# Moving a 32-column multiply from VectorE to GpSimd, and shifting a PSUM tile by eight columns

## The chip, the cores and the metric

The kernel runs on one core of a Trainium2 chip. A core has five engines that each run their own list of instructions in order and meet only through semaphores: TensorE (PE, matrix products), VectorE (DVE), ScalarE (ACT), GpSimd (POOL) and SyncE (SP, which here issues nearly all DMAs). The metric is the device time of one execution in microseconds, as a median of several; smaller is better.

## The reference

The input x is 2048 tokens by 640 features. After a layer norm without weights, two branches are added to x: a linear attention with 32 heads of 20 features ("hedgehog" feature maps), and a gated MLP of width 1536.

```python
xn = layernorm(x)
q, k, v = split(xn @ wqkv)                          # 32 heads of 20
pq, pk = q @ w_phi[h], k @ w_phi[h]                 # per head
phi_q = concat([softmax(pq), softmax(-pq)])         # 40 features per head
phi_k = concat([softmax(pk), softmax(-pk)])
kv  = sum_s phi_k[s, f] * v[s, d];   z = sum_s phi_k[s, f]
num = phi_q @ kv;   den = phi_q @ z + 1e-6
out = x + (num / den) @ wo + (silu(xn @ w1) * (xn @ w3)) @ w2
```

There is no mask: kv and z are sums over all tokens, so they must be complete before the first query is multiplied with them.

## The kernel before, in words

**Tiles.** Tokens lie in 16 tiles of 128 (index t). All matrices are bf16 and PSUM is f32: 8 banks of 512 columns, used as four pairs. `w_phi` is folded into the key and query weights first (`Wkp`, `Wqp`), so each projection gives the argument of the exponentials.

**Keys and values.** For each tile `k_tile` projects, ScalarE writes exp(p) and exp(-p) interleaved by head into `ekt`, and `k_norm` makes both softmaxes: VectorE sums the groups of 20 and takes reciprocals, GpSimd multiplies `ekt` by them in two instructions of 640 columns (`ekt<-ekt,rS`). `kv_sum` then multiplies `ekt` with v, which has a column of ones per head and so 21 columns per head, in 11 groups of up to three heads (the trace calls it `PS<-v,ekt`, 11 matmuls per tile). `kv_store` masks the result into `KVc`, 32 x 21 columns.

**Queries.** `q_proj` (`PS<-Wqp,xnT`, ten matmuls) and ScalarE's exponentials fill `eq`, where three heads of 40 features plus 8 pads make a group of 128. `q_half` (GpSimd, where the planner finds GpSimd free) adds the two halves of each softmax's terms into `half`; `q_ratio` (line 642) sums on VectorE (`Sq`: per head the sum of exp(p) and the sum of exp(-p)), takes the reciprocal of the second sum (`rq`), and multiplies it by the first, in line 650. `q_scale` (line 652) multiplies the exp(-p) terms by that ratio on GpSimd, in two instructions of 600 and 40 columns, so that both softmaxes share one denominator. A transposing DMA on SP's queue turns `eq` into `eqT`.

**The products with kv.** `q_tok` (line 664) multiplies the 11 groups of `eqT` with their 63 (last: 42) columns of `KVc`, side by side from column 0 of a pair of banks. One bank holds 512 columns and eight groups take 504, so group 8 crosses into the second bank at its eighth column. A matmul writes to one bank only, so this group is issued twice, with 8 and 55 columns: 12 matmuls per tile (`PS<-KVc,eqT`). VectorE then forms the denominator, its reciprocal and `o_tok`; SP transposes it to `oT`.

**The rest.** `mlp` (line 683) issues ten 512-column matmuls per block of 128 hidden features (`PS<-xnT,w_s`), a tanh on ScalarE (`th`), and on VectorE `t<-th,PS` and `hT<-t,PS`, both of which read the PSUM pair and so free it. `out_tile` adds `wo` and `w2` products in PSUM; VectorE adds x (`xres`) and SP stores.

**What sets the order.** The kernel writes its instruction lists with a planner. Each stage is a stream; at every turn the head of each stream is given a start time from costs written beside each operation (`cost=`), and the earliest one is committed, with its PSUM pair (`banks`, line 723) chosen by when it comes free. From then on all five lists are fixed, and waits are derived from the recorded reads and writes. A changed cost or engine anywhere can therefore reorder all that comes after it. The planner knows nothing of one engine slowing another. All operations but DMAs are issued from line 102, so the profile's rows are told apart by their tile names.

Of the kernel before, what the change touches and what calls it, by code (L numbers as in the profile page):

```python
# [4 lines left out]
ALU = mybir.AluOpType  # L5
# [5 lines left out]
H = 32  # L11
# [6 lines left out]
NG = 11  # L18
# [231 lines left out]
def bass_parallel_sum__linear_kernel_hedgehog__glu_gated_swiglu__prompt_kernel(  # L250
# [29 lines left out]
    def new(name, shape, dtype, offset=None):  # L280
        size = mybir.dt.size(dtype)
        for n in shape[1:]:
            size *= n
        return P.sbuf(name, shape, dtype, region(size) if offset is None else offset)
# [39 lines left out]
    eqT = [new(f"eqT{i}", [128, NG, 128], bf, (RKV, RE + 27648)[i // 2] + 5632 + 2816 * (i % 2)) for i in range(4)]  # L324
# [8 lines left out]
    KVc = new("KVc", [128, H * 21], bf, RW)  # L333
# [6 lines left out]
    PS = nc.alloc_psum_tensor("PS", [128, 8 * 512], f32)  # L340
# [3 lines left out]
    def bank(k, cols=512, off=0, rows=128):  # L344
        return PS[0:rows, k * 512 + off:k * 512 + off + cols]
# [5 lines left out]
    def mm(o, l, r, start, stop, shared=False, cost=None):  # L351
        n = free(r)
        P.op("PE", "matmul", [o], [l, r], (o, l, r),
             dict(start=start, stop=stop, skip_group_check=shared),
             cost=max(n / 2400 + 0.003, 0.055) if cost is None else cost)
# [5 lines left out]
    def free(ap):  # L361
        n = 1
        for s in ap.shape[1:]:
            n *= s
        return n
# [5 lines left out]
    def tt(eng, o, a, b, f, fast=1):  # L371
        c = 0.16 + free(o) / 960 / fast if eng == "DVE" else 0.2 + free(o) * 1.7 / 1000
        P.op(eng, "tensor_tensor", [o], [a, b], (o, a, b, f), cost=c)

    def stt(o, a, s, b, f0, f1):
        P.op("DVE", "scalar_tensor_tensor", [o], [a, b], (),
             dict(out=o, in0=a, scalar=s, in1=b, op0=f0, op1=f1), cost=0.16 + free(o) / 960)
# [206 lines left out]
    def group(g):  # L584
        return 3 * g, min(3, H - 3 * g)
# [46 lines left out]
    def q_sums(t):  # L632
        s = Sq[:, t % 4, :]
        i = eq[t % 4][:].rearrange("p (g c) -> p g c", c=128)[:, :, 0:120].rearrange("p g (n f) -> p g n f", f=DH)
        h = half[:, t % 2, :].rearrange("p (g n f) -> p g n f", n=6, f=10)
        return s[:, 0:66].rearrange("p (g n) -> p g n", n=6), i, h
# [5 lines left out]
    def q_ratio(t, halved):  # L642
        o, i, h = q_sums(t)
        i = h if halved else i
        P.op("DVE", "tensor_reduce", [o], [i], (o, i, AX.X, ALU.add), cost=0.12 + free(i) / 960)
        s = Sq[:, t % 4, :]
        r = rq[:, t % 3, :]
        sv = s[:, 0:64].rearrange("p (h s) -> p h s", s=2)
        P.op("DVE", "reciprocal", [r], [sv[:, :, 1]], (r, sv[:, :, 1]), cost=0.36)
        tt("DVE", r, r, sv[:, :, 0], ALU.mult)  # L650

    def q_scale(t):
        r = rq[:, t % 3, :]
# [10 lines left out]
    def q_tok(t, k):  # L664
        for g in range(NG):
            h, nh = group(g)
            c = 21 * h
            for a, b in ((c, min(c + 21 * nh, 512)), (max(c, 512), c + 21 * nh)):
                if a < b:
                    mm(bank(k, b - a, a), eqT[t % 4][:, g, :], KVc[:, a:b], a in (0, 512), b in (512, 21 * H), True,  # L670
                       max(0.026, (b - a) / 2400 + 0.003))
        p = PS[:, k * 512:k * 512 + 21 * H].rearrange("p (h c) -> p h c", c=21)
        den = den_s[:, t % 2, :]
        sv = Sq[:, t % 4, 0:64].rearrange("p (h s) -> p h s", s=2)
        stt(den, sv[:, :, 0], DEN_EPS, p[:, :, DH], ALU.mult, ALU.add)
        P.op("DVE", "reciprocal", [den], [den], (den, den), cost=0.36)
        tt("DVE", o_tok[:, t % 3, :].rearrange("p (h c) -> p h c", c=DH), p[:, :, 0:DH],
           den.unsqueeze(2).to_broadcast([128, H, DH]), ALU.mult)
# [192 lines left out]
    def q_norms():  # L871
        for t in range(T):
            while done["qp"] <= t:
                yield None
            halved = P.free["POOL"] < P.free["PE"] + 2.0
            if halved:
                yield lambda t=t: q_half(t)
            yield lambda t=t, halved=halved: q_ratio(t, halved)
            yield lambda t=t: q_scale(t)
            done["qn"] = t + 1  # L880
# [8 lines left out]
    def q_toks():  # L889
        for t in range(T):  # L890
            while done["qd"] <= t or not done["kv"]:
                yield None
            yield lambda t=t: q_tok(t, banks(2))
            done["q"] = t + 1
# [129 lines left out]
```

## Time and profile before

| | us |
|---|---|
| median of three runs (lowest, highest) | 271.44 (271.33, 271.71) |
| the profiled execution | 271.57 |
| its span in the profile | 269.8 |

Busy shares of the span: PE 98%, PE's weight loads 60%, VectorE 66%, ScalarE 37%, GpSimd 36%. The granted TensorE clock is full in all 40 slices.

How to read it: times are microseconds from the start of the span. Matmuls are pipelined and their ends are modelled, so the length shown for one (0.38 us for 512 columns) is longer than the distance from one to the next; where the pace of TensorE is wanted, starts are compared. In a row of the timeline stand start, length, engine, line, operation, output and inputs, form, and how many instructions were merged into it ("x40"); some matmul records are missing, so a merged row can say x39 where 40 were issued. A bracket at its end gives the idle time ahead of it and what ended that. Weight loads (PEld) overlap matmuls.

### The profile page before, as it was taken

Reading aid. Unit: us, or ns where it says so; the run is one execution under the profiler, and the core shown is the slowest. Engines: PE = TensorE matmul, PEld = TensorE weight load, DVE = VectorE, ACT = ScalarE, POOL = GpSimd, SP = SyncE. Lnnn points to the kernel's source line nnn. Section 1 sums busy time; section 2 is a strip of 40 time slices with the busy share of each in tenths; the row PEclk is TensorE's granted clock in tenths of the full one; section 3 lists DMA queues with packets and bytes.
Section 4 is the critical chain, followed back from the end, with each engine's and each line's share of the span. In section 5 each row is a group of like instructions: output and inputs, shape, how many; then the busy total and the mean of one; then the engine's idle time right before and its main releaser. Section 6 shows DMA issues by size and latency. Waiting matters only on the chain.

```text
span 269.8 us, 4835 instructions
## 1 busy us (share of the span) xinstructions
PE 263.6 (98%) x1958; PEld 161.9 (60%) x1978; DVE 177.9 (66%) x308; ACT 99.6 (37%) x193; POOL 97.5 (36%) x126
## 2 busy tenths in 40 slices
PE   7999999999989999999999999999999999999996
PEld 4656677776736555555555455544577777777774
DVE  4549899998899898888988878878712121212112
ACT  5547979988323434435242434242100000000000
POOL 4225848999993443644444434222000000000000
PEclk9999999999999999999999999999999999999999
DMA  6998695900093255455444460424211313131301
GB/s 193 282 309 179 147 220 116 308 10 2 4 327 72 49 102 80 80 99 102 87 80 89 91 80 10 93 57 78 49 51 52 97 49 97 51 97 49 93 31 49
DMA packets 63510, 27.73 MB, mean 103 GB/s; under 512 B 49792, under 2 KB 63488, under 8 KB 63488
## 3 DMA queue, kind: packets, MB, share of 16 engines
q1 hardware_dynamic: 63344, 27.35, 43.1%
q8 instruction: 15, 0.25, 0.4%
q10 hardware_dynamic: 144, 0.08, 0.1%
q14 instruction: 7, 0.06, 0.1%
HBM read 12.81 MB, written 2.62 MB: 57 GB/s over the span
## 4 chain that ended last, share of the span: by engine, by line
PE 74%; POOL 12%; DVE 9%; issue 3%; DMA 1%; DVEq 0%
PE PS L102 74%; POOL ekt L102 10%; DVE bst L102 4%; DVE x_tok L102 1%; POOL rstd L102 1%; DVE S L102 1%; DMA x_tok<-in_A_x_dram 1%; POOL v L102 1%; DVE hT L102 1%; DVE t L102 1%; DVE Sq L102 1%; DVE mv L102 0%; DVE rS L102 0%; POOL M L102 0%; DVE xres L102 0%
## 5 line engine op out<-in xcount | busy, mean ns | idle before, releaser
L102 PE MATMUL PS<-xnT,w_s 128*128 128x512 bf16 x463 | 105.8, 379 | 1.9 <-DVE t L102 0.8
L102 PEld LDWEIGHTS PS<-xnT,w_s 128*128 128x128 bf16 x480 | 45.5, 98 | 52.2 <-DVE t L102 1.3
L102 PE MATMUL PS<-w_s,hT 128*128 128x320 bf16 (+2 forms) x384 | 54.9, 299 | 0.0
L102 DVE TENSOR_TENSOR xres<-PS,xres 128x640 bf16<-128x640 f32 (+2 forms) x17 | 13.3, 785 | 60.0 <-PE PS L102 60.0
L102 ACT ACTIVATE th<-PS 128x512 f32<-128x512 f32 x48 | 28.8, 600 | 52.4 <-PE PS L102 52.4
L102 PEld LDWEIGHTS PS<-w_s,hT 128*128 128x128 bf16 x384 | 37.6, 98 | 14.6
L102 DVE SCALAR_TENSOR_TENSOR t<-th,PS 128x512 bf16<-128x512 f32 x48 | 32.7, 681 | 15.0 <-ACT th L102 14.6
L102 POOL TENSOR_TENSOR eq<-eq,rq 128x600 bf16<-128x600 bf16 (+1 forms) x32 | 22.6, 727 | 53.8 <-DVE rq L102 53.7
L102 POOL TENSOR_TENSOR ekt<-ekt,rS 128x640 bf16<-128x640 bf16 x32 | 39.5, 1265 | 0.6 <-DVE rS L102 0.6
L102 ACT ACTIVATE eq<-PS 128x600 bf16<-128x600 f32 (+1 forms) x72 | 24.6, 411 | 27.8 <-PE PS L102 27.6
L102 DVE SCALAR_TENSOR_TENSOR hT<-t,PS 128x512 bf16<-128x512 bf16 x48 | 33.0, 687 | 1.8 <-DVE t L102 0.2
L102 PE MATMUL PS<-wv,xnT 128*128 128x320 bf16 x160 | 24.8, 299 | 0.1
L102 PE MATMUL PS<-wo_s,oT 128*128 128x320 bf16 (+2 forms) x160 | 24.5, 299 | 0.0
L102 PE MATMUL PS<-Wkp,xnT 128*128 128x320 bf16 x160 | 23.9, 299 | 0.0
L102 ACT ACTIVATE ekt<-PS 128x640 bf16<-128x640 f32 x32 | 22.3, 703 | 3.8 <-PE PS L102 3.3
L102 PE MATMUL PS<-Wqp,xnT 128*128 128x128 bf16 (+1 forms) x157 | 23.3, 297 | 0.2
L102 DVE TENSOR_REDUCE S<-ekt 128x64 f32<-128x1280 bf16 x16 | 23.0, 1438 | 0.0
L102 POOL TENSOR_TENSOR half<-eq 128x660 f32<-128x660 bf16 x14 | 19.0, 1356 | 8.6 <-ACT eq L102 8.6
L102 PEld LDWEIGHTS PS<-wo_s,oT 128*128 128x128 bf16 x160 | 15.7, 98 | 6.3
L102 PEld LDWEIGHTS PS<-Wqp,xnT 128*128 128x128 bf16 x160 | 12.9, 98 | 10.7
L102 PEld LDWEIGHTS PS<-wv,xnT 128*128 128x128 bf16 x160 | 15.2, 98 | 6.8 <-DVE xnT L102 0.4
L102 PEld LDWEIGHTS PS<-Wkp,xnT 128*128 128x128 bf16 x160 | 15.5, 98 | 6.0
(55 smaller groups left out, 176.9 us busy)
## 6 DMA issues: line engine op xcount, KB each, us to landing
w_s<-in_B_w_dram SPq DMA_DIRECT2D x6, 640.0 KB, 6.2
xres<-in_A_x_dram SPq DMA_DIRECT2D x16, 160.0 KB, 2.3
out_dram<-xres SPq DMA_DIRECT2D x15, 160.0 KB, 1.8
x_tok<-in_A_x_dram SPq DMA_DIRECT2D x3, 640.0 KB, 6.3
w_s<-in_B_w_dram SPq DMA_DIRECT2D x1, 1920.0 KB, 8.0
wv<-in_A_wqkv_dram SPq DMA_DIRECT2D x2, 400.0 KB, 5.4
wo_s<-in_A_wo_dram SPq DMA_DIRECT2D x1, 800.0 KB, 8.4
x_tok<-in_A_x_dram SPq DMA_DIRECT2D x3, 160.0 KB, 3.3
```

The lines of the kernel that those rows point to most:

```text
L102: o = _Op(eng, lambda: m(*args, **kw), r, w, cost)
```

## The change

Two things, in two functions. In `q_ratio` the multiplication of the reciprocal by the first sum, 32 columns of f32, is issued on GpSimd and not on VectorE. In `q_tok` the output starts at column 8 of the PSUM pair and not at column 0: eight groups then end at column 512, the ninth starts the second bank, no group is split, and a tile takes 11 matmuls. VectorE reads the products from the shifted place. The planner's cost for these matmuls becomes 0.031 each (before: the larger of 0.026 and a value by columns).

```diff
     def q_ratio(t, halved):
         ...
         P.op("DVE", "reciprocal", [r], [sv[:, :, 1]], (r, sv[:, :, 1]), cost=0.36)
-        tt("DVE", r, r, sv[:, :, 0], ALU.mult)
+        tt("POOL", r, r, sv[:, :, 0], ALU.mult)
 ...
     def q_tok(t, k):
         for g in range(NG):
             h, nh = group(g)
-            c = 21 * h
-            for a, b in ((c, min(c + 21 * nh, 512)), (max(c, 512), c + 21 * nh)):
-                if a < b:
-                    mm(bank(k, b - a, a), eqT[t % 4][:, g, :], KVc[:, a:b], a in (0, 512), b in (512, 21 * H), True,
-                       max(0.026, (b - a) / 2400 + 0.003))
-        p = PS[:, k * 512:k * 512 + 21 * H].rearrange("p (h c) -> p h c", c=21)
+            a, b = 21 * h, 21 * (h + nh)
+            mm(bank(k, b - a, 8 + a), eqT[t % 4][:, g, :], KVc[:, a:b], g in (0, 8), g in (7, NG - 1), True, 0.031)
+        p = PS[:, k * 512 + 8:k * 512 + 8 + 21 * H].rearrange("p (h c) -> p h c", c=21)
```

Since the planner places everything anew, the built lists differ in more than these lines. Up to the reciprocal of the first query tile all engines' lists are the same. From there on GpSimd has 16 more multiplications (`rq<-rq,Sq`) and one more `half<-eq`: query tile 1, whose 1320 terms VectorE summed alone before, is now halved first. TensorE's list has the same projections and MLP blocks in a different order, with the 16 kv products at other places between them; SP's transposes of `eqT` and `oT` change places twice.

## The prediction

> **What bounds the kernel now.** The first view to read is the page's busy shares, then who kept TensorE waiting.
>
> ```profile
> PE 263.6 (98%) x1958; PEld 161.9 (60%) x1978; DVE 177.9 (66%) x308; ACT 99.6 (37%) x193; POOL 97.5 (36%) x126
> ...
> PE PS L102 <- DVE warm L102: 1.2, 1, 1.2
> PE PS L102 <- DVE t L102: 0.8, 1, 0.8
> PE PS L102 <- ACT Wkp L102: 0.2, 1, 0.2
> PE PS L102 <- DVE rstd L102: 0.2, 1, 0.2
> ```
>
> TensorE is the bound, and the waits on it are four. Three lie in the start-up, ahead of everything the change touches. The fourth, 0.8 us behind VectorE's `t`, is in the middle. Everything else after start-up is matmul behind matmul. So time can change in two ways only: fewer or shorter matmuls, or waits of TensorE that come or go. The third view is the timeline around that wait.
>
> ```profile
> 65.30 14.77 POOL L102 TENSOR_TENSOR ekt<-ekt,rS 128x640 bf16<-128x640 bf16 x12
> 70.82 0.63 DVE L102 SCALAR_TENSOR_TENSOR t<-th,PS 128x512 bf16<-128x512 f32 x1
> 73.51 6.42 PE L102 MATMUL PS<-xnT,w_s 128*128 128x512 bf16 x29
> 74.07 1.47 DVE L102 TENSOR_REDUCE Sq<-eq 128x66 f32<-128x1320 bf16 x1
> 74.57 0.60 ACT L102 ACTIVATE th<-PS 128x512 f32<-128x512 f32 x1 [4.90 <-PE PS L102]
> 75.57 0.35 DVE L102 RECIPROCAL rq<-Sq 128x32 f32<-128x32 f32 x1
> 75.96 4.16 DVE L102 TENSOR_TENSOR rq<-rq,Sq 128x32 f32<-128x32 f32 x1
> 80.04 0.68 DVE L102 SCALAR_TENSOR_TENSOR t<-th,PS 128x512 bf16<-128x512 f32 x1
> 80.20 1.41 POOL L102 TENSOR_TENSOR eq<-eq,rq 128x600 bf16<-128x600 bf16 x2
> 80.75 0.69 DVE L102 SCALAR_TENSOR_TENSOR hT<-t,PS 128x512 bf16<-128x512 bf16 x1
> 80.77 1.84 PEld L102 LDWEIGHTS PS<-xnT,w_s 128*128 128x128 bf16 x10 [1.33 <-DVE t L102]
> 80.78 2.33 PE L102 MATMUL PS<-xnT,w_s 128*128 128x512 bf16 x10 [0.84 <-DVE t L102]
> 82.94 1.52 PE L102 MATMUL PS<-v,ekt 128*128 128x63 bf16 x44
> ```
>
> The multiplication `rq<-rq,Sq` of query tile 0, 32 columns, takes 4.16 us. How long it takes otherwise stands here, with its neighbours:
>
> ```profile
> L102 DVE TENSOR_TENSOR rq<-rq,Sq x16: 191/192/4160, 76.0 to 181.9; 128x32 f32<-128x32 f32 x16
> ...
> L102 POOL TENSOR_TENSOR eq<-eq,rq 128x40 bf16<-128x40 bf16 x16 | 4.0, 252 | 0.0
> ...
> L102 POOL TENSOR_TENSOR rstd<-rstd 128x2 f32<-128x2 f32 x6 | 1.2, 196 | 0.5
> ```
>
> The long one begins inside GpSimd's run of twelve `ekt` multiplications and ends at 80.12, when that run is over (65.30 + 14.77 = 80.07). The sum (74.07), the reciprocal (75.57) and a `t` (70.82) ran at their usual lengths beside the same GpSimd work. What sets this instruction apart is that both its inputs lie in SBUF; `t` and `hT` have one there and one in PSUM. Behind it in VectorE's list stands the `t` of an MLP block whose tanh was ready at 75.17. It starts at 80.04, its PSUM bank comes free late, and the fourth block of the run of 40 matmuls, which needs that pair, waits.
>
> The Trainium skill, SBUF — State Buffer, "SBUF: two separate sides", has such a rule: a VectorE instruction with two SBUF inputs and a GpSimd instruction that reads SBUF exclude each other, and the later one blocks until the earlier has ended. The trace agrees on which instruction blocks, but the block outlasted three GpSimd instructions of 1.23 us (14.77/12) and not one.
>
> **The change part by part.**
>
> *VectorE's multiplication goes.* Sixteen leave VectorE: 15 x 0.19 + 4.16 = 7.0 us of its time. Fifteen of them are covered, since no matmul waits on VectorE there. The long one is not: without it the first `t` of that stretch can start at about 75.97, and its `hT` ends near 77.4. How long TensorE stood is read from starts. The pace of 512-column matmuls comes from these rows:
>
> ```profile
> 148.55 8.79 PE L102 MATMUL PS<-xnT,w_s 128*128 128x512 bf16 x39
> 157.18 0.52 PE L102 MATMUL PS<-KVc,eqT 128*128 128x63 bf16 x12
> ```
>
> 40 of them (one record is missing) take 157.18 - 148.55 = 8.63 us, 0.216 each. The 29 from 73.51 would be followed by the next at 73.51 + 29 x 0.216 = 79.77; it came at 80.78. The wait cost 1.01 us. The rows' own bounds are 0.84 (PE idle) and 1.33 (PEld idle).
>
> What is late next: the fourth block would start at 79.77 and the `v,ekt` matmuls at 79.77 + 10 x 0.216 = 81.93; their last `ekt` is ready at 80.07, so there are 1.9 us of cover. The second and third `hT` free banks for the projection at 83.3 and the block at 84.65; their tanhs end by 79.5 and VectorE does a `t` and `hT` in 1.4, so they are done by about 81. Nothing in the profile takes the wait's place; I take 1.01.
>
> *GpSimd's multiplication comes.* Its price is between 0.196 (2 columns, f32) and 0.252 (40 columns); by columns 32 lies by the latter, and I take 0.24. Sixteen are 3.9 us, and the additional `half` (1.36) makes 5.2, on an engine that is 36% busy. Behind the new instruction on GpSimd are `q_scale`'s two and the next `half`; behind those SP's transpose and then the kv products. The path from reciprocal to `q_scale` was, for tile 10:
>
> ```profile
> 141.56 0.35 DVE L102 RECIPROCAL rq<-Sq 128x32 f32<-128x32 f32 x1
> 141.94 0.19 DVE L102 TENSOR_TENSOR rq<-rq,Sq 128x32 f32<-128x32 f32 x1
> 142.21 1.42 POOL L102 TENSOR_TENSOR eq<-eq,rq 128x600 bf16<-128x600 bf16 x2 [3.62 <-DVE rq L102]
> 143.66 1.38 SPq L114 DMA_TRANSPOSE eqT<-eq  x1
> ...
> DMA to landing us min/median/max: 3.5/3.6/5.3
> ...
> 148.19 0.52 PE L102 MATMUL PS<-KVc,eqT 128*128 128x63 bf16 x12
> ```
>
> From the reciprocal's end (141.91) to `q_scale` it is 0.30. With the hop to GpSimd first (142.21 - 142.13 = 0.08), then 0.24, and a step on GpSimd of at most another 0.08, it becomes 0.32 to 0.40: up to 0.1 later. `eqT` landed at 143.66 + 3.6 = 147.26, 0.93 ahead of its matmuls. So 0.1 is hidden even here, the closest of the tiles. Had that cover gone, a tile would cost 0.1.
>
> The new order is a second risk to this cover. I count matmuls in the changed list at the paces above. For tiles 4 to 11 there lie 3 projections (10 matmuls, 1.36), 60 large matmuls and 2 kv products between a projection's start and that tile's kv product: 3 x 1.36 + 60 x 0.216 + 2 x 0.34 = 17.7 us. In the order before, tile 10 had 15.6 and still 0.93 to spare. The shortest stretch in both orders is tile 15's, 60 large matmuls with one projection and one product, 14.7 in either; there the rows of before are
>
> ```profile
> 173.93 1.52 PE L102 MATMUL PS<-Wqp,xnT 128*128 128x512 bf16 x10
> 183.65 1.39 SPq L114 DMA_TRANSPOSE eqT<-eq  x1
> 188.60 0.52 PE L102 MATMUL PS<-KVc,eqT 128*128 128x63 bf16 x12
> ```
>
> and `eqT` landed at 187.25, 1.35 early. For tile 0 the product comes at 88.16 (81.93 + 44 x 0.031 + 1.36 + 2.16 + 1.36) and not at 89.18, while GpSimd delivers 0.2 later: transposed from 81.85, landed by 85.5, 2.7 early. For tile 1, now halved on GpSimd and summed by VectorE only behind the `KVc` copies, I get: copies from 83.4 to 84.7, sum and reciprocal to 85.9, GpSimd to 87.6, landed 91.2; its product stands at 88.16 + 0.34 + 20 x 0.216 = 92.8, 1.6 early. So the order costs nothing that I can find.
>
> *One matmul less per tile.* The block of 12 takes about 0.365:
>
> ```profile
> 120.16 0.52 PE L102 MATMUL PS<-KVc,eqT 128*128 128x63 bf16 x12
> 120.53 1.52 PE L102 MATMUL PS<-Wqp,xnT 128*128 128x512 bf16 x10
> ...
> 69.22 4.24 PE L102 MATMUL PS<-v,ekt 128*128 128x63 bf16 x132
> ```
>
> The same shapes as the new block, ten of 63 and one of 42 columns, are the `v,ekt` products of a tile: 132 of them have their starts in 4.24 - 0.18 (the modelled length of the last) = 4.06, 0.031 each, so 11 take 0.34. The difference is 0.025, over 16 tiles 0.40 us, on TensorE's path throughout. Bounds: 0.02 a tile (the two parts of the split group were short ones), 0.32; and a full 0.031, 0.50.
>
> *Sum.* Against the profiled execution, 271.57: 271.57 - 1.01 - 0.40 = 270.16. Outside the span lie 271.57 - 269.8 = 1.8 us, which nothing touches. The median of the runs is 0.13 lower than the profiled one, so 270.0 to 270.2; I say 270.1. With the bounds of both terms, 0.84 + 0.32 and 1.33 + 0.50, and the median as reference, it is 269.6 to 270.4.
>
> **The rivals.**
>
> *The wait stays.* If VectorE was held by something else than this instruction's inputs, the next one in its list would be held instead, and only the matmuls' 0.4 remains: 271.44 - 0.4 = 271.0, no change that can be measured. Against it: three other kinds of VectorE instructions ran beside the same GpSimd work.
>
> *A smaller new wait.* The lists are placed anew by costs that knew nothing of the 4.16 us, and a kv product or a bank may come up to 0.9 late once or twice in 16 tiles: 270.4 to 270.9. For it: margins of 0.93 exist. Against it: TensorE had no other wait in the old order, made from the same costs.
>
> *Slower: the chain through GpSimd.* The multiplication now stands in GpSimd's list ahead of `q_scale`, and each tile's transpose hangs on it. It decides once the chain is more than the margin longer, that is when the small multiplication takes over 0.93 + 0.19 = 1.1 us or so. As long as GpSimd's 640-column one (1.23), it would make tiles with that margin wait 0.2; were all sixteen so close, 3 us, and the time 271.4 - 1.4 + 3 = 273. For it: GpSimd is slow per instruction. Against it: its rows of 0.196 and 0.252, and longer stretches in the new order. The Trainium skill, GPSIMD Engine Reference, "Engine selection", speaks against the change: elementwise work belongs on VectorE, GpSimd being about twice as slow with two inputs. By that rule the instruction takes 2 x 0.19 = 0.38, an estimate from the page, and the chain would be 0.2 longer, still under the margin of 0.93; the sum would be the same.
>
> **How the numbers follow.** A measurement of this kernel can tell about 0.2%, 0.54 us, from no change (its three runs span 0.38). Wait gone and no new one: 0.77, at 270.1 (269.6 to 270.4). A smaller new wait: 0.08, also faster. The wait stays: 0.06, same. Slower by the chain, or by a late bank of that order: 0.09. Faster is 0.85. The range reaches from 269.6 to the smaller new wait's end, 270.9, and leaves 0.15 out.
>
> **What would show it.** Right: no `rq` on VectorE, 16 on GpSimd of 0.2 to 0.3 us; no row of VectorE over 2 us; no wait of TensorE behind `t`; 11 kv matmuls in 0.34 us; the last matmul group starting 1.4 us earlier. Wrong: a wait of TensorE behind `eqT`, `KVc` or `hT` after 76 us; a `t` at 76 that takes 4 us; or `rq` on GpSimd of a microsecond.

## The result, and the profile after

| | before | after |
|---|---|---|
| median of six runs (lowest, highest), us | 271.40 (271.21, 271.71) | 269.91 (269.55, 270.20) |
| profiled execution, us | 271.57 | 269.55 |
| its span, us | 269.8 | 267.8 |

The ratio is 0.9944, with a 95% interval of 0.9931 to 0.9957: faster by 1.49 us (0.6%), as forecast in sign, in size (270.1 was said) and, as the rest shows, in its two causes.

First the busy shares of the changed kernel:

```profile
PE 263.9 (99%) x1962; PEld 161.7 (60%) x1962; DVE 171.0 (64%) x292; ACT 99.5 (37%) x193; POOL 102.9 (38%) x143
```

and all waits of TensorE in it (total, times, longest):

```profile
PE PS L102 <- DVE warm L102: 1.2, 1, 1.2
```

The wait behind `t` is no longer there; what is left is the very first wait of the start-up. VectorE lost 6.9 us of busy time (7.0 was worked out), GpSimd gained 5.4 (5.2). The timeline of the same stretch as before:

```profile
72.67 8.79 PE L102 MATMUL PS<-xnT,w_s 128*128 128x512 bf16 x40
74.95 0.35 DVE L102 RECIPROCAL rq<-Sq 128x32 f32<-128x32 f32 x1
75.22 0.63 DVE L102 SCALAR_TENSOR_TENSOR t<-th,PS 128x512 bf16<-128x512 f32 x1
79.41 0.25 POOL L102 TENSOR_TENSOR rq<-rq,Sq 128x32 f32<-128x32 f32 x1
79.73 1.41 POOL L102 TENSOR_TENSOR eq<-eq,rq 128x600 bf16<-128x600 bf16 x2
81.30 1.51 PE L102 MATMUL PS<-v,ekt 128*128 128x63 bf16 x44
87.53 0.50 PE L102 MATMUL PS<-KVc,eqT 128*128 128x63 bf16 x11
87.87 4.48 PE L102 MATMUL PS<-xnT,w_s 128*128 128x512 bf16 x20
...
263.85 1.47 PE L102 MATMUL PS<-w_s,hT 128*128 128x256 bf16 x12
```

`t` follows the reciprocal at once, while GpSimd's run goes on until 79.4, and the 40 large matmuls run through: 81.30 - 72.67 = 8.63 us. A kv product takes 87.87 - 87.53 = 0.34.

That the profiled executions are 2.02 us apart and the medians 1.49 is the start-up: the 40 matmuls begin at 72.67 here and at 73.29 before (the first of them had lost its record: 73.51 - 0.216), 0.62 earlier, ahead of anything the change touches. From there to the last group of matmuls it is 263.85 - 72.67 = 191.18 us and was 265.86 - 73.29 = 192.57 (before, that group is the row below). The change is worth the difference, 1.39 us.

```profile
265.86 1.47 PE L102 MATMUL PS<-w_s,hT 128*128 128x256 bf16 x12
```

### The profile page after: what moved, and what is told of

Same layout as the page of the kernel before. It is cut to its first block, busy times and chain, and to the rows that moved or that the text cites. A ratio compares the mean times of both kernels' runs of the same rounds, so it can differ in the third digit from the quotient of the medians.

```text
span 267.8 us, 4821 instructions
## 1 busy us (share of the span) xinstructions
PE 263.9 (99%) x1962; PEld 161.7 (60%) x1962; DVE 171.0 (64%) x292; ACT 99.5 (37%) x193; POOL 102.9 (38%) x143
## 4 chain that ended last, share of the span: by engine, by line
PE 97%; DVE 1%; DMA 1%; POOL 0%; issue 0%
PE PS L102 97%; DMA x_tok<-in_A_x_dram 1%; DVE bst L102 0%; POOL rstd L102 0%; DVE x_tok L102 0%; DVE xres L102 0%; DVE mv L102 0%; DVE rstd L102 0%
## 5 line engine op out<-in xcount | busy, mean ns | idle before, releaser
L102 PE MATMUL PS<-xnT,w_s 128*128 128x512 bf16 x480 | 107.5, 379 | 0.0
L102 PE MATMUL PS<-Wqp,xnT 128*128 128x512 bf16 (+1 forms) x160 | 24.1, 299 | 0.0
L102 POOL TENSOR_TENSOR rq<-rq,Sq 128x32 f32<-128x32 f32 x16 | 4.0, 252 | 48.8 <-DVE rq L102 48.8
L102 POOL TENSOR_TENSOR half<-eq 128x660 f32<-128x660 bf16 x15 | 20.4, 1358 | 3.6 <-ACT eq L102 3.6
```

What stands on the lines that cost most here:

```text
L102: o = _Op(eng, lambda: m(*args, **kw), r, w, cost)
```

## The experiments

Each time stands beside the median of runs of the kernel before that were taken with it; these medians lie between 271.02 and 271.25. Where a kernel ran once, the lengths in its trace carry the argument more than its time does.

### Each part alone

The multiplication on GpSimd, the kv products as before:

```diff
         P.op("DVE", "reciprocal", [r], [sv[:, :, 1]], (r, sv[:, :, 1]), cost=0.36)
-        tt("DVE", r, r, sv[:, :, 0], ALU.mult)
+        tt("POOL", r, r, sv[:, :, 0], ALU.mult)
```

> The multiplication on GpSimd, the kv products still from column 0 with 12 matmuls a tile. My theory (the long VectorE instruction held one MLP block back by 1.01 us): no wait of TensorE behind t, 12 matmuls in 0.365 us, time 271.4 - 1.0 = 270.4, whatever new order the lists get. Rival (the wait passes to the next VectorE instruction, and the gain of the whole change comes from elsewhere): the first t after the reciprocal takes 4 us, time 271.4. Rival (the new order, and not the wait, made the gain): the wait is gone but the time is off 270.4 by more than 0.5.

Measured: 270.03 us (five runs, 269.84 to 270.42) against 271.14, ratio 0.9961 (0.9949 to 0.9974), 1.1 us less. TensorE's wait behind `t` is gone, the 12 matmuls keep their 0.365. The rivals of this run fall.

The other part alone, `q_tok` as changed and the multiplication on VectorE:

```diff
-            c = 21 * h
-            for a, b in ((c, min(c + 21 * nh, 512)), (max(c, 512), c + 21 * nh)):
...
+            a, b = 21 * h, 21 * (h + nh)
+            mm(bank(k, b - a, 8 + a), eqT[t % 4][:, g, :], KVc[:, a:b], g in (0, 8), g in (7, NG - 1), True, 0.031)
+        p = PS[:, k * 512 + 8:k * 512 + 8 + 21 * H].rearrange("p (h c) -> p h c", c=21)
```

> The output from column 8 and 11 matmuls a tile, the multiplication still on VectorE. All other engines' lists keep the order of before. My theory: the 4.2 us instruction and the 1.0 us wait of TensorE stay, 11 matmuls in 0.34 us, time 271.4 - 0.4 = 271.0. Rival (a matmul pair costs its weight load, 0.098 us): 16 x 0.098 = 1.6 less, 269.8. Rival (the short matmuls were free): 271.4.

Measured: 270.74 us (eleven runs) against 271.14, ratio 0.9987 (0.9978 to 0.9996), 0.4 us less. Its row among the waits of TensorE:

```profile
PE PS L102 <- DVE t L102: 0.9, 1, 0.9
```

and its timeline:

```profile
75.49 4.17 DVE L102 TENSOR_TENSOR rq<-rq,Sq 128x32 f32<-128x32 f32 x1
...
88.71 0.50 PE L102 MATMUL PS<-KVc,eqT 128*128 128x63 bf16 x11
89.05 2.10 PE L102 MATMUL PS<-xnT,w_s 128*128 128x512 bf16 x9
```

The long instruction and the wait behind it stay, and 11 matmuls take 89.05 - 88.71 = 0.34. A pair does not cost its weight load of 0.098, and it is not free. The two parts add up: 1.1 and 0.4 against 1.49 for both.

### What holds VectorE's product

Only the instruction in that one place exchanged, for query tile 0. This kernel leaves out the multiplication of that tile's ratio:

```diff
-        tt("DVE", r, r, sv[:, :, 0], ALU.mult)
+        if t == 0:
+            P.op("DVE", "reciprocal", [r], [r], (r, r), cost=0.16 + H / 960)
+        else:
+            tt("DVE", r, r, sv[:, :, 0], ALU.mult)
```

> Before, with one instruction exchanged: for query tile 0 VectorE takes a second reciprocal of rq instead of the product, so that tile's ratio is left out (its output is wrong); the same place in the list, one SBUF input and not two, all orders as before. My theory (two SBUF inputs against GpSimd's run): the second reciprocal takes 0.35 us, t follows at once, TensorE does not wait, time 271.4 - 1.0 = 270.4, with the other fifteen products still on VectorE. Rival (VectorE is held at that place whatever it issues): the second reciprocal or the t behind it takes 4 us, time 271.4.

Measured: 270.15 us (five runs) against 271.14, ratio 0.996 (0.9947 to 0.9974). Its timeline:

```profile
75.58 0.35 DVE L102 RECIPROCAL rq<-rq 128x32 f32<-128x32 f32 x1
75.85 0.63 DVE L102 SCALAR_TENSOR_TENSOR t<-th,PS 128x512 bf16<-128x512 f32 x1
...
79.66 2.56 POOL L102 TENSOR_TENSOR eq<-eq,rq 128x600 bf16<-128x600 bf16 x3
80.38 0.52 DVE L102 TENSOR_TENSOR rq<-rq,Sq 128x32 f32<-128x32 f32 x1
```

In the middle of the same GpSimd run, an instruction with one SBUF input takes 0.35 us and the wait of 1.0 us is gone, with all lists in the order of before. So it is the product and not the place, and one instruction of the sixteen carried the whole gain of the move to GpSimd. The last row is a find: the next tile's product now falls beside `q_scale` and takes 0.52, not 0.19 and not four microseconds. It ended at 80.90; the 600-column instruction that it met, by its group's mean of 1.20 us, at about 80.86. Here it got in after one GpSimd instruction.

The operation, or its inputs? The same product in the operation that `t` and `hT` use:

```diff
-        tt("DVE", r, r, sv[:, :, 0], ALU.mult)
+        stt(r, r, 1.0, sv[:, :, 0], ALU.mult, ALU.mult)
```

> Before, with VectorE's product written as scalar_tensor_tensor (times 1.0, times the sum): the same two SBUF inputs, another operation, the same lists. My theory: it is blocked as the plain product was, 4.1 to 4.2 us for tile 0, TensorE waits 1.0, time 271.4. Rival (it is this operation, tensor_tensor, that GpSimd excludes, since t and hT are scalar_tensor_tensor and were not held): about 0.2 us for tile 0, time 270.4.

Measured: 271.16 us (one run) beside 271.14, and

```profile
75.57 4.16 DVE L102 SCALAR_TENSOR_TENSOR rq<-rq,Sq 128x32 f32<-128x32 f32 x1
```

`t` ran beside GpSimd in the same operation with one input in PSUM. In these runs, both inputs in SBUF is what makes an instruction wait.

How long? Two more multiplications at the end of GpSimd's run:

```diff
             tt("POOL", ev, ev, r[:, 32 * q:32 * q + 32].unsqueeze(2).to_broadcast([128, 32, DH]), ALU.mult)
+        if t == T - 1:
+            for q in range(2):
+                P.op("POOL", "tensor_tensor", [half[:, q, 0:640]], [ekt[:, t * 2 * D:t * 2 * D + 640]],
+                     (half[:, q, 0:640], ekt[:, t * 2 * D:t * 2 * D + 640], ekt[:, t * 2 * D:t * 2 * D + 640], ALU.mult), cost=0.0)
```

> Before, with two more GpSimd multiplications of 640 columns (ekt of the last tile with itself into half, not used) behind the last softmax multiplication, so that GpSimd's unbroken run is 2.5 to 2.7 us longer; all other lists as before. If VectorE's product is held until the run has ended: it takes 4.2 + 2.6 = 6.8 us, TensorE's wait behind t grows from 1.0 to about 3.6, time 274. If it is held until one GpSimd instruction ends, or for a time of its own: 4.2 us as before, the wait 1.0, time 271.4 to 271.6.

Measured: 275.44 us (one run) beside 271.25, in its timeline:

```profile
73.11 6.63 PE L102 MATMUL PS<-xnT,w_s 128*128 128x512 bf16 x30
75.82 6.58 DVE L102 TENSOR_TENSOR rq<-rq,Sq 128x32 f32<-128x32 f32 x1
79.87 2.48 POOL L102 TENSOR_TENSOR half<-ekt 128x640 f32<-128x640 bf16 x2
83.06 3.57 PE L102 MATMUL PS<-xnT,w_s 128*128 128x512 bf16 x10 [3.31 <-DVE t L102]
86.42 1.93 PE L102 MATMUL PS<-v,ekt 128*128 128x63 bf16 x44
88.19 2.88 PE L102 MATMUL PS<-Wqp,xnT 128*128 128x512 bf16 x20
```

The product ended at 82.40 and GpSimd's run at 82.35. It is held for as long as this run goes on; one GpSimd instruction, or a time of its own, is out. The time rose by 4.2 us and not by 2.6. The wait became 3.47 by starts (73.11 + 30 x 0.216 = 79.59, and the next came at 83.06), 2.46 more than 1.01. The rest is TensorE's pace after it: ten large matmuls took 86.42 - 83.06 = 3.36 instead of 2.16, the 44 small ones 1.77 instead of 1.36. The busy-by-window view gives the granted clock (the third number from the end of a row; behind it stand the DMA share and the rate):

```profile
83.06:84.00 0.94, 0.94 (x5) 0.47 (x6) 0.94 (x2) 0.00 (x0) 0.84 (x2) 1.00 0.00 0
84.00:87.00 3.00, 3.00 (x18) 1.37 (x17) 2.90 (x5) 0.60 (x1) 0.00 (x0) 0.50 0.63 120
87.00:87.50 0.50, 0.50 (x15) 0.50 (x13) 0.50 (x2) 0.00 (x0) 0.33 (x1) 0.59 0.00 0
87.50:88.00 0.50, 0.50 (x22) 0.50 (x19) 0.47 (x2) 0.00 (x0) 0.50 (x1) 1.00 0.00 0
```

When TensorE went on after its pause of 3.5 us, the clock stayed full for 0.9 us, was then at half for about 3.4 us (84.0 to 87.4), and was full again. After the 1.0 us pause of the kernel before it stayed full (1.00 from 80.78 to 84). One run shows this, so how long a pause may be is not known from here.

What lets the product in? Something short between GpSimd's last six long multiplications, first a memset:

```diff
             tt("POOL", ev, ev, r[:, 32 * q:32 * q + 32].unsqueeze(2).to_broadcast([128, 32, DH]), ALU.mult)
+            if t >= 13:
+                P.op("POOL", "memset", [warm[:, 0:4]], [], (warm[:, 0:4], 0.0), cost=0.0)
```

> Before, with a memset of 4 columns (it reads nothing from SBUF) behind each of GpSimd's last six softmax multiplications; all other lists as before. VectorE's product still meets the run. If it is let in as soon as GpSimd runs something that does not read SBUF: it takes at most about 0.6 us (from its start to the end of the multiplication under way), TensorE's wait behind t is gone, time 270.4. If the run of GpSimd as a whole keeps it out, whatever stands in it: about 4.5 us (the run is some 0.1 longer per memset left), the wait 1.3, time 271.7.

then a multiplication of 32 columns of a constant that is no longer used:

```diff
+            if t >= 13:
+                d = BDc[:, 0, 0:H]
+                P.op("POOL", "tensor_tensor", [d], [d], (d, d, GM[:, 0, 0:H], ALU.mult), cost=0.0)
```

> The same with a multiplication of 32 columns (it reads SBUF) in place of each memset. VectorE's product got in after one GpSimd instruction where q_scale's 40-column instruction came next (0.52 us, in the run with the second reciprocal). If a short instruction behind a long one is what lets it in: at most 0.6 us, no wait of TensorE, 270.4. If it is kept out by any unbroken run of instructions that read SBUF: 4.16 plus 3 x 0.25, about 4.9 to 5.2 us, the wait 1.8 to 2, time 272.2 to 272.5.

Measured: 271.25 us and 270.60 (one run each) beside 271.02. The two timelines, memset first:

```profile
75.45 4.36 DVE L102 TENSOR_TENSOR rq<-rq,Sq 128x32 f32<-128x32 f32 x1
75.90 0.10 POOL L102 MEMSET warm<- 128x4 f32 x1
75.96 1.27 POOL L102 TENSOR_TENSOR ekt<-ekt,rS 128x640 bf16<-128x640 bf16 x1
...
78.49 1.27 POOL L102 TENSOR_TENSOR ekt<-ekt,rS 128x640 bf16<-128x640 bf16 x1
79.70 0.10 POOL L102 MEMSET warm<- 128x4 f32 x1
```

```profile
75.62 1.29 POOL L102 TENSOR_TENSOR ekt<-ekt,rS 128x640 bf16<-128x640 bf16 x1
76.08 0.88 DVE L102 TENSOR_TENSOR rq<-rq,Sq 128x32 f32<-128x32 f32 x1
76.85 0.27 POOL L102 TENSOR_TENSOR BDc<-BDc,GM 128x32 bf16<-128x32 bf16 x1
76.89 0.68 DVE L102 SCALAR_TENSOR_TENSOR t<-th,PS 128x512 bf16<-128x512 f32 x1
...
81.34 2.61 POOL L102 TENSOR_TENSOR eq<-eq,rq 128x600 bf16<-128x600 bf16 x3
81.46 1.16 DVE L102 TENSOR_TENSOR rq<-rq,Sq 128x32 f32<-128x32 f32 x1
```

A memset between two long multiplications did not let the product in (4.36 us; TensorE waited 1.0 by its row, 0.84 before). Whether a memset alone holds it is not shown; the product ended at 79.81, 0.05 behind the last long multiplication (78.49 + 1.27 = 79.76), the same lag as without memsets, and 0.01 behind the last memset (79.80). The small multiplication let the product in: it ended at 76.96, just behind the long multiplication it had met (76.91), and TensorE did not wait behind `t`. The time is only 0.4 under that of the one run of the kernel before beside it. The trace leaves the start-up out: from the first of the 40 matmuls (73.57 - 0.216, since its record is missing) to the last group (264.90) it is 191.55 us, 1.02 less than the 192.57 of before, the whole wait. The next tile's product met `q_scale` here too and took 1.16, ending behind the 600-column instruction, with the 40-column one next. So in all three meetings a boundary between a long GpSimd multiplication and a short one let VectorE in, and a boundary between two long ones did not, in any of the runs where the product met them. Why this is so is not settled; a memset's boundary is not enough.

### How deep the cover of the longer chain is

Idle multiplications on GpSimd behind each `rq`, in the changed kernel; n is 3, 8 and 5:

```diff
         tt("POOL", r, r, sv[:, :, 0], ALU.mult)
+        for _ in range(n):
+            d = BDc[:, 0, 0:H]
+            P.op("POOL", "tensor_tensor", [d], [d], (d, d, GM[:, 0, 0:H], ALU.mult), cost=-0.03)
```

> The changed kernel with three idle multiplications of 32 columns on GpSimd behind each rq product, all lists otherwise as in the changed kernel. Each step costs about 0.32 with its wait (start of rq to start of q_scale is 0.33 in the changed kernel), so every query tile's transpose comes 1.0 us later. My theory (the chain is hidden by its margins; by issue time plus 3.6 us the closest tile, 15, has 1.2): no wait of TensorE, 269.9. Rival (the chain is already close to the path): some 16 x 0.1 or more is added, 271.5 and over.

Measured: 270.11 us (four runs) against 271.25: 1.14 less, where the changed kernel was 1.49 less. The main reading holds, with one wait that I had not expected, ahead of tile 12's product (0.36 by starts), here in the timeline:

```profile
161.88 0.51 PE L102 MATMUL PS<-KVc,eqT 128*128 128x63 bf16 x11 [0.20 <-DMA eqT<-eq]
```

and this is the landing of that tile's transpose alone, in the view of the tile `eqT`:

```profile
DMA to landing us min/median/max: 5.3/5.3/5.3
```

The 5.3 is not the median of 3.6 that I had used for all tiles. In the changed kernel the same transpose takes 5.2; its product stands 0.93 - 0.36 = 0.57 us behind it (by that kernel's own rows, 161.29 - 155.56 - 5.2 = 0.53). Tile 12 and not 15 is the closest.

> The same with eight, every tile's transpose 2.6 us later. By the margins (tile 1: 1.6, tile 2: 2.5, tile 11: 1.6, tile 12: 2.1, tile 15: 1.2; the others 2.6 to 3.5): waits of TensorE ahead of the kv products of tiles 1, 11, 12 and 15 of 1.0, 1.0, 0.5 and 1.4 us less what earlier waits give back, together 2 to 4 us, time 272 to 274. Rival (the chain is hidden far deeper than the margins say): no wait, 269.9.

Measured: 278.14 us (one run) beside 271.25. "No wait" falls, and so does my sum. In its timeline:

```profile
121.28 0.50 PE L102 MATMUL PS<-KVc,eqT 128*128 128x63 bf16 x11 [0.51 <-DMA eqT<-eq]
122.86 1.42 POOL L102 TENSOR_TENSOR eq<-eq,rq 128x600 bf16<-128x600 bf16 x2
124.24 1.36 POOL L102 TENSOR_TENSOR half<-eq 128x660 f32<-128x660 bf16 x1
125.63 0.84 DVE L102 TENSOR_REDUCE Sq<-half 128x66 f32<-128x660 f32 x1 [1.60 <-POOL half L102]
126.51 0.35 DVE L102 RECIPROCAL rq<-Sq 128x32 f32<-128x32 f32 x1
126.94 0.26 POOL L102 TENSOR_TENSOR rq<-rq,Sq 128x32 f32<-128x32 f32 x1 [1.34 <-DVE rq L102]
127.15 2.52 POOL L102 TENSOR_TENSOR BDc<-BDc,GM 128x32 bf16<-128x32 bf16 x8
127.98 0.50 PE L102 MATMUL PS<-KVc,eqT 128*128 128x63 bf16 x11 [0.53 <-DMA eqT<-eq]
129.63 1.42 POOL L102 TENSOR_TENSOR eq<-eq,rq 128x600 bf16<-128x600 bf16 x2
```

From one tile's `q_scale` to the next it is 129.63 - 122.86 = 6.77 us, and no step in it waits for anything outside: each tile's `half` stands in GpSimd's list behind the `q_scale` of the tile before, VectorE's sum waits for it, and `rq` for that. TensorE's share of a tile is 6.02 (1.36 + 20 x 0.216 + 0.34). Once the loop is the longer one, tile after tile waits: the products of tiles 4 to 11 come 6.7 to 6.9 us apart (here 127.98 - 121.28 = 6.70), and margins no longer count there. The run between the two tests that:

> The changed kernel with five idle multiplications, between the two tried. With eight, the loop half, sum, reciprocal, rq, idle ones, q_scale, next half took 6.76 us a tile against 6.02 that TensorE needs for one, and each tile waited anew. If that loop is the cause of the steep loss: at five it takes 6.76 - 3 x 0.31 = 5.83, under 6.02, and only single margins are overdrawn, by a shift of 1.55: tile 12 by 1.0 (with three idle ones it waited 0.36 at a shift of 0.93, so its margin is 0.57), tile 15 by 0.3, tile 1 by 0.1; about 1.4 in all, 271.4. If the loss simply grows with what is added (0.4 us at three, 8.4 at eight): some 3.6, 273.6.

Measured: 270.87 us (ten runs, 270.50 to 271.73) against 271.18, ratio 0.9989 (0.9978 to 1.0). That is 0.31 less, where the changed kernel was 1.49 less, so 1.2 dearer than that kernel (1.0 by the bare times, 270.87 against 269.91). Its timeline:

```profile
155.34 6.63 PE L102 MATMUL PS<-xnT,w_s 128*128 128x512 bf16 x30
162.58 0.51 PE L102 MATMUL PS<-KVc,eqT 128*128 128x63 bf16 x11 [0.60 <-DMA eqT<-eq]
...
179.27 6.63 PE L102 MATMUL PS<-xnT,w_s 128*128 128x512 bf16 x30
186.00 0.51 PE L102 MATMUL PS<-KVc,eqT 128*128 128x63 bf16 x11
```

TensorE waits ahead of the products of tiles 12 and 15, by 0.76 and 0.25 us by starts (thirty matmuls of 0.216 ahead of each), and at no other tile. That is close to the 1.4 of the loop reading, and far from 3.6.

## Why the prediction was right, point by point

*VectorE's multiplication goes, 1.01 us.* Right in size and cause. The second reciprocal shows that one instruction is the price, the other operation that its inputs are, the longer run that TensorE's wait follows its length. The Trainium skill, SBUF — State Buffer, "SBUF: two separate sides", names the right pair of instructions. On the duration the runs differ: by the Trainium skill it is one GpSimd instruction; it was one where a short multiplication followed (0.52, 0.88 and 1.16 us), and all that were left of the run elsewhere (4.16 to 6.58). In the same section the Trainium skill also says that a GpSimd instruction that reads no SBUF does not block such a VectorE instruction. In the run with memsets the last of them fits this, since the product ended 0.05 behind the last long multiplication, as it does without memsets; but memsets between long multiplications did not let it in (4.36 us).

*What is late next: nothing.* Right. No wait came in its place, and the `v,ekt` matmuls, at 81.30, found their last `ekt` ready.

*One matmul less, 0.40 us.* Right: 0.4 in time alone, 0.34 against 0.365 a tile. The rest of 1.39, after 1.01, is 0.38, or 0.024 a tile.

*GpSimd's multiplication, 0.24 us each.* It takes 0.252; the start of `q_scale` comes 0.32 behind that of `rq`. The chain is hidden, as said. The step that was wrong is its cover: I took the closest tile from issue plus the median landing, 0.93 before and 1.35 for tile 15 in the new order. A transpose that lands in 5.2 leaves tile 12 only 0.57. In the kernel before, too, tile 7 was closer than tile 10, with 0.8 (issued at 125.54, landed 3.7 later, its product at 130.07). The error cost nothing, since 0.1 was added, but the margin was about half of what I said.

*The range.* Its upper end, 270.4, is not worked out from the median, as I said it was: 271.44 - 0.84 - 0.32 = 270.3, while 270.4 comes from the profiled execution, 271.57. The measured 269.91 lies inside either way.

*The rival "the wait stays"* fell with the first run. *"Slower"* was put at a small multiplication of over 1.1 us; the first wait does come at 0.9 more, but there the kernel is still faster than before (270.11 against 271.25), and at 1.55 more the gain is nearly used up (270.87 against 271.18). A loss as steep as my "3 us" came with the loop, not with the margins: eight idle ones (2.5 us) cost 8.4 against the changed kernel (278.14 - 271.25 + 1.49). *"A smaller new wait"* did not come.

## What to carry to other kernels

An instruction of 32 columns can cost a microsecond on the engine that bounds a kernel, if it has both inputs in SBUF on VectorE and meets a long run of GpSimd multiplications: look for the maximum in a group's durations, not its mean, and follow what stands behind it. To get rid of the wait, move that instruction to GpSimd's own list, which took it away here; an instruction with one SBUF input in its place was not held either. When a chain off the path is made longer, check each tile's own landing time, and then the loop from tile to tile: an overdrawn margin is paid at that tile alone, while a loop that is longer than a tile on the bounding engine is paid in tile after tile.

## What the runs showed of the hardware

Three things were not expected. GpSimd's run of long multiplications keeps a VectorE instruction with two SBUF inputs out across as many as six of its instructions (6.58 us), a memset of 0.10 us between them does not open it, and a multiplication of 32 columns does. After a pause of TensorE of 3.5 us the granted clock was full for 0.9 us and then 0.50 for about 3.4 us, which made a wait of 2.5 us more cost 4.2. And single DMA transposes of equal size took 3.5 to 5.3 us from issue to landing.
